# Casting q, k and v on ScalarE in layer 2, and loading the last tokens one tail ahead, in a sliding-window attention with an MLP

## The chip, the core and the metric

The kernel runs on one core of one Trainium2 chip. The metric is the time of one execution on the device in microseconds (us). The core has five engines, each with an instruction stream of its own that it runs in order: TensorE (PE in the profile; its weight loads are shown as PEld), VectorE (DVE), ScalarE (ACT), GpSimd (POOL) and SyncE (SP), which here only issues DMA transfers. Streams meet only where one waits for another's semaphore.

## The reference

Batch 8, 8 heads, 576 positions, head size 64, in float32. Attention looks back over a window of 64 positions; its result, with the heads side by side (512 columns), is normalised and goes through a two-layer MLP of hidden size 2048, with a residual.

```
scores = (q @ k^T) / sqrt(64);  keep 0 <= i - j < 64, else -1e9
x      = softmax(scores) @ v                         # [8, 8, 576, 64] -> [8, 576, 512]
xn     = (x - mean(x)) / sqrt(var(x) + 1e-6) * g_ln
out    = x + relu(xn @ w_ch1) @ w_ch2                # 512 -> 2048 -> 512
```

## The kernel before

**Groups and periods.** The positions 0 to 511 of each batch row are one group (g = 0 to 7), four blocks of 128 tokens each. The last 64 positions of each row, the tails, are put together as a ninth group (g = 8): block i of it, "tail i", holds the last 64 tokens of rows 2i and 2i + 1. A loop over g runs the MLP of group g while the attention of group g + 1 is worked out and the inputs of group g + 2 are loaded, cast to float16 and transposed. One turn of the loop is called a period here. Periods 2 to 5 are the steady ones; in periods 6 and 7 there is no further full group to prepare, and the tails are prepared and attended to instead. Period 8 is the MLP of the tails alone.

**Units and slots.** From period 2 on, the MLP of a group is 30 units on TensorE. Units 0 to 15 are layer 1: four matmuls of 128x512 (`hps`), and a Relu on ScalarE that writes `hrT`. Units 16 to 29 are layer 2, done with seven products of half-size blocks (`product`, n = 1, 2, 6, 5, 7, 3, 4, two token halves each) into the banks X, Y and Z, with sums of `hrT` prepared by VectorE (`presum`, the tiles `sw`) and added into the output tile `osb` by VectorE (`post`). X is used four times in a row, so each time TensorE waits until VectorE has read it. All other work is hung behind a unit with `at(unit, function, arguments)`: after each unit the functions in its slot are called, and the order of these calls is the order of the instructions on every engine. Nothing reorders them afterwards, except that the engines run apart as far as semaphores allow.

**Attention steps in the slots.** `s_mm(g, j)` does the scores of block j on TensorE, followed (or one unit later) by two exps on ScalarE; `s_mask` multiplies the mask in on VectorE; `b_step` multiplies by v on TensorE and does the division and the statistics on VectorE; `r_step` does 1/sqrt(var + eps) as two small instructions on ScalarE; `z_step` normalises on VectorE; `x_step` transposes z into `zT` by a DMA transpose from SP's queue, and `zt_step` does the same on TensorE. The next period's layer 1 reads `zT`.

**Inputs.** `load_qk` and `load_v` issue the loads of group g + 2 from SP at the start of period g. `cast_q` and `cast_v` cast them on GpSimd, one instruction for each half of q and of k (128x1024) and one for each quarter of v (128x512). To keep GpSimd from running them too early, `pace(t)` puts a one-column copy of some tile in front, so that the cast waits for that tile. In the steady periods the casts of q and k stand in slots 3, 5, 8 and 10, those of v in 18, 20, 22 and 25. `x_main` transposes the cast q and k, half by half, by three DMA transposes from SP each, in slots 13 and 22. `make_vB` copies v with a shift of 64 positions by two DMAs from GpSimd. The float32 buffers of q and k (`qk32_0`, `qk32_1`) are two deep, that of v (`v32`) one deep.

**Tails.** `load_tail(i)` loads q, k and v of tail i in six DMAs, q, k, v for each of its two rows, into the same buffers. `cast_tail` casts them on GpSimd in three parts (q, k, v), paced; `x_tail` transposes q and k by one DMA transpose each. The table `TAILS` gives the slots: tail 0 is loaded in slot 0 of period 6, and the load of tail i + 1 stands in the slot of `x_tail(i)`, behind it.

Of the kernel before, what the change touches and what calls it, by code (L numbers as in the profile page):

```python
# [10 lines left out]
FP32 = mybir.dt.float32  # L11
# [7 lines left out]
def kernel(  # L19
# [10 lines left out]
    nc = tc.nc  # L30
# [3 lines left out]
    SM = 512  # L34
# [60 lines left out]
    def load_tail(i):  # L95
        tq = p_in.tile([128, H, D], FP32, tag="qk32_0", name=f"tq32_{i}")
        tk = p_in.tile([128, 2, H, D], FP32, tag="qk32_1", name=f"tk32_{i}")
        tv = p_in.tile([128, 2, H, D], FP32, tag="v32", name=f"tv32_{i}", bufs=1)
        tail32[i] = (tq, tk, tv)
        for r in range(2):  # L100
            b = 2 * i + r
            nc.sync.dma_start(out=tq[64 * r:64 * r + 64], in_=q[b, :, SM:S, :].rearrange("h s d -> s h d"))
            nc.sync.dma_start(out=tk[:, r], in_=k[b, :, S - 128:S, :].rearrange("h s d -> s h d"))
            nc.sync.dma_start(out=tv[:, r], in_=v[b, :, S - 128:S, :].rearrange("h s d -> s h d"))

    def cast_tail(i, part):
        if part == 0:
            tail16[i] = (p_in.tile([128, H, D], FP16, tag="qk16_0", name=f"tq16_{i}"),
                         p_in.tile([128, 2, H, D], FP16, tag="qk16_1", name=f"tk16_{i}"))
            nc.gpsimd.tensor_copy(out=tail16[i][0], in_=tail32[i][0])  # L110
        elif part == 1:
            nc.gpsimd.tensor_copy(out=tail16[i][1], in_=tail32[i][1])
        else:
            vt = p_va.tile([128, 2, H, D + 1], FP16, tag=("vA", "vB")[i % 2], name=f"vt_{i}")
            vT[i] = vt
            nc.gpsimd.memset(vt[:, :, :, D:D + 1], 1.0)
            nc.gpsimd.tensor_copy(out=vt[:, :, :, 0:D], in_=tail32.pop(i)[2])
# [5 lines left out]
    def cast_q(b, x, half):  # L123
        t = qk32.pop((b, x, half))
        dst = p_in.tile([128, 8, 2, D], FP16, tag=f"qk16_{x}", name=f"qk16_{x}_{b}_{half}")
        qk16[(b, x, half)] = dst
        if b >= NPE and x == 1:
            nc.gpsimd.tensor_copy(out=dst[:, :].rearrange("p a e d -> p (a e d)"), in_=t)
            return
        j = 2 if b < 2 else 4  # L130
        nc.gpsimd.tensor_copy(  # L131
            out=dst[:, :].rearrange("p (a j) e d -> p a e j d", j=j),
            in_=t[:, :].rearrange("p (a e j d) -> p a e j d", e=2, j=j, d=D),
        )
# [14 lines left out]
    def cast_v(b, c0, c1):  # L149
        nc.gpsimd.tensor_copy(out=vA[b][:, c0:c1, :, 0:D], in_=v32[b][:, c0:c1])  # L150
# [494 lines left out]
    def rest_of_loads():  # L645
        for i in range(8):
# [13 lines left out]

    TAILS = {
        6: ((0, load_tail, 0), (8, cast_tail, 0), (13, x_tail, 0), (13, load_tail, 1), (21, cast_tail, 1),
            (24, x_tail, 1), (24, load_tail, 2), (21, s_mm, 8, 0), (22, s_mask, 8, 0), (26, b_step, 8, 0)),
        7: ((0, x_step, 8, 0), (0, s_mm, 8, 1), (2, s_mask, 8, 1), (4, b_step, 8, 1), (7, x_step, 8, 1),
            (1, cast_tail, 2), (6, x_tail, 2), (6, load_tail, 3), (9, s_mm, 8, 2), (11, s_mask, 8, 2),
            (13, b_step, 8, 2), (16, x_step, 8, 2), (13, cast_tail, 3), (17, x_tail, 3),
            (20, s_mm, 8, 3), (21, s_mask, 8, 3), (24, b_step, 8, 3), (28, zt_step, 8, 3)),
    }
    for g in range(NGRP):
# [18 lines left out]
        def steps(bg, bj, ub, us, sg, sj):  # L688
            if us is not None:
                score(us, bg, bj)  # L690
            late = ub < 15
            at(ub, b_step, bg, bj)
            if sj < 4:
                score(ub, sg, sj)
            at(ub + 1 + late, r_step, bg, bj)
            at(ub + 2, z_step, bg, bj)
            at(ub + 3, x_step, bg, bj)
# [78 lines left out]
        for i, f, *p in TAILS.get(g, ()):  # L776
# [10 lines left out]
            elif f is cast_tail:  # L787
                for part in range(3):
                    u = i + (0, 1, 3)[part]
                    if u < 16:  # L790
                        at(u, lambda u=u: pace(hrTs[g][:, u, 0:1]))
                    elif part == 1:
                        at(u, lambda: pace(rss[(b, 3)]))
                    at(u, cast_tail, p[0], part)
            else:
                at(i, f, *p)
        if 0 < g and b + 1 < B:
# [19 lines left out]
            else:  # L817
                at(3, alloc_qkT, n)
                for u, x, half in ((3, 0, 0), (5, 1, 0), (8, 0, 1), (10, 1, 1)):
                    at(u, lambda u=u: pace(hrTs[g][:, u, 0:1]))  # L820
                    at(u, cast_q, n, x, half)
                at(13, x_main, n, 0)
                at(22, x_main, n, 1)
                at(18, alloc_v, n)
                at(18, alloc_vB, n)
                for u, c, t in ((18, 0, lambda: rss[(b, 2)]), (20, 1, lambda: oo_of[g][0][:, 0, 0:1]),
                                (22, 2, lambda: rss[(b, 3)]), (25, 3, lambda: oo_of[g][1][:, 0, 256:257])):
                    at(u, lambda t=t: pace(t()))
                    at(u, cast_v, n, c, c + 1)
                at(26, make_vB, n)  # L830
# [37 lines left out]
```

## Time and profile before

| | |
|---|---|
| runs | 325.7, 330.42, 326.16, 333.08 us; median 328.29 us |
| the profiled execution | 325.7 us, of which the span from first to last instruction is 324.0 us |
| mean granted clock of TensorE | 0.973 |
| busy: PE | 297.2 us (92%) |
| busy: PEld | 186.6 us (58%) |
| busy: DVE | 201.9 us (62%) |
| busy: ACT | 158.6 us (49%) |
| busy: POOL | 130.8 us (40%) |
| DMA | 61.55 MB, mean 190 GB/s |
| casts of q and k on POOL (L131, L128) | 32 of 128x1024, 1073 and 1109 ns each |
| casts of v on POOL (L150) | 32 of 128x512, 783 ns each |

Shares are of the span. Matmuls are pipelined, so a busy PE isn't a PE at its peak. A row such as `PE sc L284 <- DMA tkT<-tk: 6.9, 2, 4.2` reads: the instructions of PE that write `sc`, in line 284, waited for a DMA from `tk` to `tkT`, 6.9 us in all, two times, the longest 4.2 us. Tiles are named without their buffer numbers: `hps` and `hrT` are layer 1's sums and result, `sc` the scores, `pt` their exps, `xps` the product with v, `rs` the 1/sqrt, `z` the normalised tokens, `tqT` and `tkT` the transposed q and k of a tail. "Granted clock" is the share of TensorE's full clock that it was given.

### The profile page before, as it was taken

Reading aid. Unit: us, or ns where it says so; the run is one execution under the profiler, and the core shown is the slowest. Engines: PE = TensorE matmul, PEld = TensorE weight load, DVE = VectorE, ACT = ScalarE, POOL = GpSimd, SP = SyncE. Lnnn points to the kernel's source line nnn. Section 1 sums busy time; section 2 is a strip of 40 time slices with the busy share of each in tenths; the row PEclk is TensorE's granted clock in tenths of the full one; section 3 lists DMA queues with packets and bytes.
Section 4 is the critical chain, followed back from the end, with each engine's and each line's share of the span. In section 5 each row is a group of like instructions: output and inputs, shape, how many; then the busy total and the mean of one; then the engine's idle time right before and its main releaser. Section 6 shows DMA issues by size and latency. Waiting matters only on the chain.

```text
span 324.0 us, 7255 instructions
## 1 busy us (share of the span) xinstructions
PE 297.2 (92%) x2907; PEld 186.6 (58%) x2907; DVE 201.9 (62%) x348; ACT 158.6 (49%) x325; POOL 130.8 (40%) x215
## 2 busy tenths in 40 slices
PE   5779998999999989999998999999999949599993
PEld 2446443866744567458645764685478425485582
DVE  0655319377876994698389829973898416371361
ACT  2699751765938801870385048406831725106600
POOL 3676755942754435352435343542504143001000
PEclk9899999999999999999999999999999968789999
DMA  7999899999989857997999699969989996303005
GB/s 178 253 369 342 301 281 264 300 274 241 160 178 281 145 75 171 323 183 119 191 294 188 113 190 292 183 133 252 145 163 149 283 159 94 67 0 131 0 2 130
DMA packets 140002, 61.55 MB, mean 190 GB/s; under 512 B 117072, under 2 KB 132944, under 8 KB 139968
## 3 DMA queue, kind: packets, MB, share of 16 engines
q1 hardware_dynamic: 135792, 49.17, 73.0%
q0 software_dynamic: 3216, 11.39, 12.1%
q10 hardware_dynamic: 960, 0.53, 0.6%
q8 instruction: 23, 0.38, 0.5%
q14 instruction: 11, 0.09, 0.1%
HBM read 38.80 MB, written 9.44 MB: 149 GB/s over the span
## 4 chain that ended last, share of the span: by engine, by line
PE 62%; DVE 14%; DMA 6%; ACT 6%; issue 5%; SPq 5%; POOL 1%; POOLq 0%; DVEq 0%
PE hps L429 23%; PE wX L505 12%; PE wZ L505 7%; PE hph L466 5%; DMA qk<-in_q_dram 4%; PE ch L442 4%; DVE z L357 3%; PE sc L284 3%; PE ch L480 3%; PE xps L327 3%; DVE stats L335 2%; DVE xn L333 2%; DVE sw L419 2%; DVE osb L520 2%; DMA tkT<-tk 2%
## 5 line engine op out<-in xcount | busy, mean ns | idle before, releaser
L429 PE MATMUL hps<-zT,w1g 128*128 128x512 f16 x480 | 113.3, 385 | 0.1
L433 ACT ACTIVATE hrT<-hps 128x512 f16<-128x512 f32 x120 | 71.5, 596 | 59.3 <-PE hps L429 50.8
L429 PEld LDWEIGHTS <-w1g 128*128 128x128 f16 x480 | 45.3, 99 | 54.0 <-issue 7.0
L505 PEld LDWEIGHTS <-sw 128*128 128x128 f16 x448 | 44.6, 100 | 11.8 <-issue 5.4
L311 DVE TENSOR_TENSOR pt<-pt,mask 128x1024 f16<-128x1024 f16 x32 | 24.5, 766 | 31.0 <-ACT pt L304 18.6
L505 PEld LDWEIGHTS <-hrT 128*128 128x128 f16 x336 | 32.4, 98 | 5.4
L346 ACT ACTIVATE rs<-mv,epst 128x1 f32<-128x1 f32 x36 | 10.7, 298 | 46.2 <-DVE mv L337 46.2
L131 POOL CAST qk<-qk 128x1024 f16<-128x1024 f32 x22 | 23.5, 1073 | 22.6 <-DMA qk<-in_q_dram 18.4
L357 DVE TENSOR_SCALAR z<-xn,mv,rs 128x512 f16<-128x512 f32 x32 | 25.7, 802 | 4.5 <-ACT rs L347 4.3
L419 DVE TENSOR_TENSOR sw<-hrT 128x1024 f16<-128x1024 f16 x28 | 20.7, 740 | 11.5 <-ACT hrT L433 11.5
L390 POOL DMA_DIRECT2D out_dram<-osb x20 | 13.2, 663 | 34.7 <-DVE osb L520 23.3
L150 POOL CAST vA<-v 128x512 f16<-128x512 f32 x32 | 24.9, 783 | 2.5 <-DMA v<-in_v_dram 2.4
L335 DVE BATCH_NORM_STATS2 stats<-xn 128x6 f32<-128x512 f32 x36 | 25.0, 695 | 1.2
L333 DVE TENSOR_TENSOR xn<-xps,rcp 128x512 f32<-128x512 f32 x36 | 24.9, 691 | 1.2
L304 ACT ACTIVATE pt<-sc 128x512 f16<-128x512 f32 x32 | 17.4, 595 | 15.7 <-PE sc L284 15.3
L298 ACT ACTIVATE pt<-sc 128x512 f16<-128x512 f32 x40 | 23.8, 594 | 1.8 <-PE sc L284 0.4
L363 POOL CAST tok<-hrT 128x1 f32<-128x1 f16 x28 | 9.3, 331 | 37.4 <-ACT hrT L433 34.2
L466 PE MATMUL hph<-zT,w1g 128*128 128x256 f16 x192 | 23.9, 273 | 0.4 <-ACT zT L374 0.2
L520 DVE TENSOR_TENSOR osb<-wX,xn 128x512 f32<-128x512 f32 x21 | 14.4, 686 | 11.7 <-PE wX L505 11.7
L327 PEld LDWEIGHTS <-pt 128*64 128x64 f16 x576 | 12.3, 111 | 14.3 <-issue 5.7
L466 PEld LDWEIGHTS <-w1g 128*128 128x128 f16 x192 | 17.8, 98 | 3.9 <-issue 0.8
L442 PE MATMUL ch<-w2s,hrT 128*128 128x512 f16 x80 | 19.8, 380 | 0.0
(80 smaller groups left out, 402.9 us busy)
## 6 DMA issues: line engine op xcount, KB each, us to landing
qk<-in_q_dram SPq DMA_DIRECT2D x16, 512.0 KB, 8.4
v<-in_v_dram SPq DMA_DIRECT2D x32, 256.0 KB, 6.0
w2s<-in_moe_w_ch_dram SPq DMA_DIRECT2D x12, 512.0 KB, 7.6
out_dram<-osb POOLq DMA_DIRECT2D x12, 512.0 KB, 6.3
qk<-in_k_dram SPq DMA_DIRECT2D x20, 256.0 KB, 7.8
qk<-in_k_dram SPq DMA_DIRECT2D x6, 512.0 KB, 6.9
w1s<-in_moe_w_ch_dram SPq DMA_DIRECT2D x4, 512.0 KB, 7.2
out_dram<-osb POOLq DMA_DIRECT2D x8, 256.0 KB, 6.0
```

The lines of the kernel that those rows point to most:

```text
L150: nc.gpsimd.tensor_copy(out=vA[b][:, c0:c1, :, 0:D], in_=v32[b][:, c0:c1])
L298: nc.scalar.activation(out=pt[:, par].rearrange("k h w (p j) -> k (h w) p j", j=4), in_=sc[:, :].rearrange("k h w (j p) -> k (h w) p j", j=4),
L311: nc.vector.tensor_tensor(out=ptv, in0=ptv, in1=mb, op=ALU.mult)
L333: nc.vector.tensor_tensor(out=xn, in0=xps[:, :, 0:D], in1=rcp_b, op=ALU.mult)
L335: nc.vector.bn_stats(out=stats, in_=xn.rearrange("p h d -> p (h d)"))
L357: nc.vector.tensor_scalar(out=z, in0=x, scalar1=mv[:, 0:1], scalar2=rss[(g, kb)][:, 0:1], op0=ALU.subtract, op1=ALU.mult)
L419: nc.vector.tensor_tensor(out=S[i], in0=a, in1=b, op=op)
L429: nc.tensor.matmul(out=hps, lhsT=w1g[:, kc, 128 * hc:128 * (hc + 1)], rhs=zT[g][:, kc, :], start=(kc == KCS[0]), stop=(kc == KCS[-1]),)
L433: nc.scalar.activation(out=hrT[:, hc, :], in_=hps, func=AF.Relu, bias=0.0, scale=1.0)
L442: nc.tensor.matmul(out=ch[kb], lhsT=hrT[:, hc, 128 * kb:128 * (kb + 1)], rhs=w2s[:, hc, :], start=(hc == 0), stop=(hc == NHC - 1),)
L466: nc.tensor.matmul(out=hps[:, e], lhsT=w1g[:, kc, 128 * hc:128 * (hc + 1)], rhs=zT[g][:, kc, 256 * half:256 * half + 256], start=(kc == KC ...
L505: nc.tensor.matmul(out=xyz[bank][:, t], lhsT=lhsT, rhs=rhs, start=bool(first and t == 0 and hc == 0), stop=(t == 1 and hc == 7), skip_grou ...
```

## The change

In the steady periods (2 to 5) the casts of q, k and v are issued to ScalarE (`nc.scalar.copy`) instead of GpSimd, without `pace`, and in other slots: q and k in 16, 16, 17 and 19, v in 21 to 24. `x_main` goes to the slots 18 and 21, `make_vB` to 25. Of block 3 of each group, `r_step` and `z_step` stand one slot later.

For the tails, `load_tail` is split: part 0 loads q and k (first both rows of q, then both of k), part 1 loads v. The loads are hung one tail further ahead: q and k of tail 1 stand in slot 6 of period 6, before `x_tail(0)` in slot 10; those of tail 2 in slot 15, before `x_tail(1)` in 18; those of tail 3 in slot 23, before `x_tail(2)` in 25. The casts of tails 1 and 2 go to ScalarE in layer 2 of period 6; those of tails 0 and 3 stay on GpSimd, paced. Two blocks of tail scores, `s_mm(8, 0)` and `s_mm(8, 1)`, stand in period 6 (slots 15 and 27) instead of one, and the last tail's `zt_step` on TensorE becomes an `x_step`.

```diff
+    def load_tail(i, part):
+        if part == 0:
+            tail32[i] = (p_in.tile([128, H, D], FP32, tag="qk32_0", name=f"tq32_{i}"),
+                         p_in.tile([128, 2, H, D], FP32, tag="qk32_1", name=f"tk32_{i}"))
+            tq, tk = tail32[i]
+            for r in range(2):
+                nc.sync.dma_start(out=tq[64 * r:64 * r + 64], in_=q[2 * i + r, :, SM:S, :].rearrange("h s d -> s h d"))
+            for r in range(2):
+                nc.sync.dma_start(out=tk[:, r], in_=k[2 * i + r, :, S - 128:S, :].rearrange("h s d -> s h d"))
+        else:
+            tv = p_in.tile([128, 2, H, D], FP32, tag="v32", name=f"tv32_{i}", bufs=1)
+            tail32[i] += (tv,)
+            for r in range(2):
+                nc.sync.dma_start(out=tv[:, r], in_=v[2 * i + r, :, S - 128:S, :].rearrange("h s d -> s h d"))
...
+    def cp(act, out, in_):
+        if act:
+            nc.scalar.copy(out=out, in_=in_)
+        else:
+            nc.gpsimd.tensor_copy(out=out, in_=in_)
...
     TAILS = {
-        6: ((0, load_tail, 0), (8, cast_tail, 0), (13, x_tail, 0), (13, load_tail, 1), (21, cast_tail, 1),
-            (24, x_tail, 1), (24, load_tail, 2), (21, s_mm, 8, 0), (22, s_mask, 8, 0), (26, b_step, 8, 0)),
-        7: ((0, x_step, 8, 0), (0, s_mm, 8, 1), (2, s_mask, 8, 1), (4, b_step, 8, 1), (7, x_step, 8, 1),
-            (1, cast_tail, 2), (6, x_tail, 2), (6, load_tail, 3), (9, s_mm, 8, 2), (11, s_mask, 8, 2),
-            (13, b_step, 8, 2), (16, x_step, 8, 2), (13, cast_tail, 3), (17, x_tail, 3),
-            (20, s_mm, 8, 3), (21, s_mask, 8, 3), (24, b_step, 8, 3), (28, zt_step, 8, 3)),
+        6: ((0, load_tail, 0, 0), (0, load_tail, 0, 1), (6, load_tail, 1, 0), *tail_casts(0, False, 8, 9, 10),
+            (10, x_tail, 0), (10, load_tail, 1, 1), *tail_casts(1, True, 16, 17, 18), (18, x_tail, 1),
+            (15, s_mm, 8, 0), (16, s_mask, 8, 0), (26, b_step, 8, 0),
+            (15, load_tail, 2, 0), (21, load_tail, 2, 1), (23, load_tail, 3, 0),
+            *tail_casts(2, True, 24, 25, 26), (25, x_tail, 2),
+            (27, s_mm, 8, 1), (28, s_mask, 8, 1)),
+        7: ((0, x_step, 8, 0), (1, load_tail, 3, 1), (2, b_step, 8, 1), (2, s_mm, 8, 2), (4, s_mask, 8, 2),
+            (5, x_step, 8, 1), (7, b_step, 8, 2), (10, x_step, 8, 2), *tail_casts(3, False, 5, 6, 8), (8, x_tail, 3),
+            (12, s_mm, 8, 3), (14, s_mask, 8, 3), (17, b_step, 8, 3), (20, x_step, 8, 3)),
     }
...
-            at(ub + 1 + late, r_step, bg, bj)
-            at(ub + 2, z_step, bg, bj)
+            at(ub + 2, r_step, bg, bj)
+            at(ub + 2 + (not late), z_step, bg, bj)
...
-                for u, x, half in ((3, 0, 0), (5, 1, 0), (8, 0, 1), (10, 1, 1)):
-                    at(u, lambda u=u: pace(hrTs[g][:, u, 0:1]))
-                    at(u, cast_q, n, x, half)
-                at(13, x_main, n, 0)
-                at(22, x_main, n, 1)
+                for u, x, half in ((16, 0, 0), (16, 1, 0), (17, 0, 1), (19, 1, 1)):
+                    at(u, cast_q, n, x, half, True)
+                at(18, x_main, n, 0)
+                at(21, x_main, n, 1)
...
-                for u, c, t in ((18, 0, lambda: rss[(b, 2)]), (20, 1, lambda: oo_of[g][0][:, 0, 0:1]),
-                                (22, 2, lambda: rss[(b, 3)]), (25, 3, lambda: oo_of[g][1][:, 0, 256:257])):
-                    at(u, lambda t=t: pace(t()))
-                    at(u, cast_v, n, c, c + 1)
-                at(26, make_vB, n)
+                for c in range(4):
+                    at(21 + c, cast_v, n, c, c + 1, True)
+                at(25, make_vB, n)
```

## The prediction

> **What bounds the kernel now.** I began with the 40-slice table of the page. TensorE is busy in nearly every slice except two near the end, and there its clock drops as well:
>
> ```profile
> PE   5779998999999989999998999999999949599993
> PEclk9899999999999999999999999999999968789999
> ```
>
> So TensorE sets the time, and there is a hole. Next came the table by stage, cut at the first `hps` matmul of each period g (g=2 to g=8; columns: length, busy time of PE, PEld, DVE, ACT, POOL, clock, DMA share, GB/s):
>
> ```profile
> 95.48:127.07 31.59, 30.11 (x306) 19.23 (x304) 25.31 (x43) 14.74 (x32) 14.05 (x23) 1.00 0.83 168
> 127.07:157.04 29.97, 29.67 (x304) 19.05 (x302) 22.18 (x39) 14.66 (x32) 12.90 (x24) 1.00 1.00 203
> 157.04:188.70 31.66, 30.26 (x308) 19.37 (x306) 23.54 (x39) 14.55 (x32) 13.72 (x24) 1.00 0.91 201
> 188.70:219.62 30.92, 30.07 (x307) 19.20 (x304) 23.48 (x39) 14.66 (x32) 14.23 (x24) 1.00 0.98 202
> 219.62:250.22 30.60, 30.60 (x337) 19.61 (x335) 24.13 (x44) 16.21 (x36) 8.60 (x14) 1.00 1.00 179
> 250.22:292.32 42.10, 34.30 (x279) 20.83 (x277) 20.19 (x35) 14.34 (x30) 8.64 (x16) 0.84 0.61 119
> ```
>
> Period 7 takes 42.1 us with fewer PE instructions than period 6, which takes 30.6 and has no idle time. Periods 2 to 5 lose 1.48, 0.30, 1.40 and 0.85 us, 4.0 together. The waits of PE name the two causes:
>
> ```profile
> PE sc L284 <- DMA tkT<-tk: 6.9, 2, 4.2
> PE wX L505 <- DVE osb L520: 3.9, 7, 1.0
> ```
>
> The first is the scores of a tail waiting for its transposed keys. The second is the X bank of layer 2 waiting for VectorE. The timeline shows the first (its SP queue, then PE):
>
> ```profile
> 261.31 1.23 SPq L254 DMA_TRANSPOSE tkT<-tk  x1
> 262.60 0.62 SPq L102 DMA_DIRECT2D tq<-in_q_dram  x1
> 264.44 0.61 PE L284 MATMUL sc<-tqT,tkT 64*128 64x64 f16 x16 [4.21 <-DMA tkT<-tk]
> 281.01 0.61 PE L284 MATMUL sc<-tqT,tkT 64*128 64x64 f16 x16 [2.73 <-DMA tkT<-tk]
> ```
>
> Tail i+1 is loaded only behind the transposes of tail i, so load, cast and transpose of one tail follow each other within one tail's time.
>
> **What the change removes in the tail.** The waits are 4.21 + 2.73 = 6.94 us. After each the granted clock is 0.50: in the two-microsecond windows from 264.4 to about 269.2, and from 281.0 to about 286.3. A wide matmul there takes 0.43 us instead of 0.21, so half of 4.8 and half of 5.3 is lost: 5.05. Sum 12.0. Check: period 6 has five score and five value groups (0.41 and 0.45 us), period 7 three of each, so period 7 should last 30.6 - 2 x 0.86 = 28.9; it lasts 13.2 more, which also holds 0.86 of waiting for VectorE. Moving `s_mm(8, 1)` from period 7 to 6 only moves PE work. `zt_step(8, 3)` (four transposes on PE, 0.39 us) becomes a DMA transpose issued at unit 20; `zT` transposes land in 3.4 us and ten units of some 0.9 remain, so it is covered and PE gains 0.4. Without that cover it would cost up to its 3.4.
>
> **What it moves in the steady periods.** Four q/k casts and four v casts leave GpSimd for ScalarE. No row has the very cast on ScalarE. The nearest are a 1024-wide copy (1008 ns), a 64-partition f32-to-f16 cast of 512 (619), and a 512-wide cast with a per-partition scale (722). I take 1.0 and 0.62: 4 x 1.0 + 4 x 0.62 = 6.5 us a period; bounds 6.4 and, by doubling 722, 4 x 1.45 + 4 x 0.72 = 8.7. What hides them is ScalarE's idle time in layer 2:
>
> ```profile
> 212.02 0.29 ACT L346 ACTIVATE rs<-mv,epst 128x1 f32<-128x1 f32 x1 [5.34 <-DVE mv L337]
> 220.73 0.60 ACT L433 ACTIVATE hrT<-hps 128x512 f16<-128x512 f32 x1 [8.19 <-PE hps L429]
> ```
>
> q0, k0, q1 (3.0, at most 4.4) go into the 5.34; k1 and v (3.5, at most 4.3) into the 8.19. Cost zero. Behind them on ScalarE wait `r_step` of block 3, then z on VectorE, then the X bank: if q0 to q1 took over 5.3 us, the excess would go to PE. On SP, `x_main(n, 0)` moves from unit 13 to 18, past the zT transpose of block 2; `x_main(n, 1)` from 22 to 21, still behind that of block 3. Each is three DMA transposes of some 1.26 us on SP. In period 5 SP was held by loads until 205.3 and reached `x_main(n, 0)` only at 209.2; the casts on ScalarE, starting behind the last Relu at 206.7, give k0 at 208.7 (all four halves had landed: the last q/k cast ran at 204.6). So SP's order is new but its times are not: 209.9 to 213.7 for the first half, z of block 3 to 215, then the second, where 215.8 was. `make_vB` on GpSimd now waits for the last v cast (216.1 instead of 217.9), and the output stores behind it go no later. The r and z steps of block 3 go one unit later, z behind one `sw` of 0.69 instead of ahead of it: nothing, as both stand ahead of the same `osb`.
>
> **What the moved casts free.** VectorE is slowed while GpSimd casts:
>
> ```profile
> 168.41 1.04 POOL L128 CAST qk<-qk 128x1024 f16<-128x1024 f32 x1 [0.92 <-DMA qk<-in_k_dram]
> 168.76 1.24 DVE L419 TENSOR_TENSOR sw<-hrT 128x1024 f16<-128x1024 f16 x1
> 231.22 0.66 DVE L419 TENSOR_TENSOR sw<-hrT 128x1024 f16<-128x1024 f16 x1
> ```
>
> The second and third are the same operation, with a cast beside it and without. z takes 0.86 in the mean of periods 2 to 5 and 0.55 alone: 16 x 0.31 = 4.9 us, and `sw` and the masks add some 3.7. PE can get back only what it lost, 4.0 in all. Period 6, where no cast stands beside layer 2 until late, lost nothing, so I take most of it, 3.0; bounds 0 (VectorE would still be late) and 4.0.
>
> **New waits in the tail, the part that costs.** These are estimates on period 6's own times.
> 1. SP now has ten loads in period 6 (tail 0, then q and k of tail 1) ahead of `x_tail(0)`. Six took 221.2 to 228.4, 1.2 each; the later six 0.78 each. Ten take 7.8 to 12: until 229 to 233. Then z of block 0 (1.3), tqT and tkT (1.25 each), and 3.1 to land: tkT at 235.0 to 239.0. `s_mm(8, 0)` is now at unit 15, 236.6. Wait: 0 to 2.4; I take 1.0.
> 2. v of tail 1 is loaded behind that, lands near 242.5, and its cast (1.0) is ahead of `r_step(7, 3)` on ScalarE, which was at 241.8. About 1.7 late, most of it inside wait 1 and PE's lead: 0.5, bounds 0 and 2.
> 3. v of tail 2 goes out behind the zT transpose of block 3 (244.7 to 246.4), two issues of 0.6, 5.3 to land: 251 to 253. Its cast stands on ScalarE ahead of r of (8, 0), the two exps of `s_mm(8, 1)` and the first Relu of period 7, 1.0 + 0.5 + 1.1 us of work; that Relu was at 251.5 and comes at 253.5 to 255.5. PE has two banks of lead, 1.8 us, and its own delay of 1.5. I take 1.5; bounds 0 and 3.
>
> Sum 3.0, bounds 0 and 7.4. `s_mm(8, 2)` and `(8, 3)` follow their transposes by about 2 and 0.8 us by the same reckoning: zero, but thin for the last.
>
> Here a threshold matters. The trace has PE at half clock after a wait of 2.73 us, which followed 0.86 of idling; waits up to 1.0 in the steady periods left it at 1.00. I price a lone wait under 2.7 at its length only. The Trainium skill, "TensorE: Matmul & The Clock Gate", Part 1, puts the drop at an idle window of about 3.4 us. By it only waits of that length would be charged the 2.65 of half clock, and the sum would be the same 3.0; the row is stricter, and I let the row decide in the rivals.
>
> **Sum.** 324.0 - 12.0 - 0.4 - 3.0 + 3.0 = 311.6 us of span. The profiled execution took 325.7, 1.7 around its span: 313.3. The median of the four runs (325.7 to 333.08) lies 2.6 above that execution, so the predicted median is 315.9.
>
> **Rivals.**
> - Forecast, 316: chance 0.64. Own range 308.4 (4.0 regained, no new wait, the 0.86 of period 7 gone too, no offset of the median) to 320.3 (new waits 7.4).
> - The tail wait is moved, not removed: one new wait, tkT of tail 0 or of tail 3, passes 2.7 and halves the clock, adding some 3 + 2.65. Speaking for it: 0.8 of slack at tail 3. Against: every tail has half a period more. 316 + 5.7 = 321.6. Chance 0.21, half of it past the 2% line.
> - Slower: the second q half comes late in every steady period. Its transpose was issued at 215.8, takes 3.3 to land (219.1) and is read at 220.6: 1.5 us of slack. If the casts on ScalarE or SP's new order delay it by more than 1.5, PE waits at unit 0. A delay of 4.5 gives 3 of wait and 2.65 at half clock in each of four periods, 22.6: 338.5. It beats the gain in the tail from 3.1 a period on. Against: SP reached it by loads, not by casts. Chance 0.11.
> - The change doesn't shorten the tail: loads of one tail ahead crowd the DMA (share 1.35 around 230) and land as late as before. Only the 3.0 and 0.4 remain: 324.9. Against: the DMA share is 0.20 to 0.32 from 232 to 236. Chance 0.04.
>
> A run can tell about 2% of this kernel from no change, so faster means under 321.7. Faster: 0.64 + 0.11 = 0.75; same: 0.10 + 0.04 = 0.14; slower 0.11. The range, 308.4 to 325.0, adds the moved wait and the tail that isn't shortened to the forecast's own.
>
> **What will show it.** Right: period 7 near 30 us, clock 1.00 through it, `tkT` gone from PE's waits, z near 0.55. Wrong: a wait of `sc` for `qkT` at unit 0, `rs` late behind a cast, or `hrT` of period 7 waiting for a v load. The forecast falls if period 7 still shows clock 0.5, or if periods 2 to 5 exceed 31 us.

## The result, and the profile after

The changed kernel takes 321.75 us (median of 12 runs, 320.57 to 324.47). The kernel before took 326.16 in the same comparison (17 runs). The ratio is 0.990 (95% interval 0.986 to 0.994): the change gains 1.0%, where 3.8% was forecast (315.9 against 328.29). The time lies inside the range given, but the gain is under the 2% that the forecast named as its line. Here and below a median is of all executions, while a ratio and its interval leave out those more than 1.5% above the fastest of the same kernel. The profiled execution took 320.86 us, of which 319.1 are its span, at a mean granted clock of 0.982.

The 40-slice table of the changed kernel has the same two rows as before:

```profile
PE   6689999999999999999799979999958979999993
PEclk9999999999999999999999989999995999999999
```

The two lean slices of period 7 are gone; lean ones stand earlier, in period 6, and the clock has its gap there, with a small dent (8) before it. The table by stage tells where each piece is. Columns as before: length, busy time of PE, PEld, DVE, ACT, POOL, clock, DMA share, GB/s; one row for each of the periods 2 to 7.

```profile
93.50:123.70 30.20, 29.84 (x305) 19.22 (x304) 23.28 (x43) 20.56 (x40) 3.08 (x7) 1.00 0.88 178
123.70:154.60 30.90, 29.89 (x306) 19.21 (x305) 21.68 (x40) 20.56 (x40) 3.68 (x8) 1.00 0.96 201
154.60:185.20 30.60, 29.94 (x305) 19.41 (x306) 20.29 (x38) 20.66 (x40) 3.35 (x7) 1.00 1.00 203
185.20:218.60 33.40, 31.34 (x306) 19.73 (x305) 20.98 (x39) 20.77 (x40) 3.48 (x8) 0.95 0.98 193
218.60:257.00 38.40, 33.84 (x354) 21.33 (x352) 24.15 (x44) 21.12 (x43) 5.39 (x12) 0.91 1.13 190
257.00:287.70 30.70, 28.66 (x259) 18.50 (x258) 19.32 (x34) 13.60 (x29) 6.25 (x10) 1.00 0.51 104
```

Against the rows of before, period 7 fell by 11.40 us (42.10 to 30.70), as forecast. Period 6 grew by 7.80 (30.60 to 38.40). Periods 2 to 5 changed by -1.39, +0.93, -1.06 and +2.48, 0.96 longer in all, where 3.0 less was forecast. Period 8 is 0.28 shorter. Another 1.98 lies ahead of period 2, in code that is the same; there, profiled executions of the unchanged code differ by as much (period 2 starts at 93.6 and at 95.5 in two kernels with it). The sum is 4.9, the difference of the spans.

PE's waits name what came in:

```profile
PE sc L292 <- DMA tkT<-tk: 6.6, 3, 4.6
PE sc L292 <- DMA qkT<-qk: 2.7, 2, 2.1
PE hps L437 <- DMA zT<-z: 1.0, 1, 1.0
PE wX L513 <- DVE osb L528: 0.4, 1, 0.4
```

The last row is the relief of VectorE: the X bank waited 3.9 us in seven places before, and 0.4 in one now. The first three rows were not there or were elsewhere, and all three are DMA transposes. Of the waits for `tkT`, 4.56 us stand in period 6, for tail 0, and 2.0 in period 7, in two places.

The timeline of period 6 shows the first wait, from SP's queue (rows marked SPq) to TensorE:

```profile
219.88 2.29 SPq L101 DMA_DIRECT2D tq<-in_q_dram  x2
...
230.14 1.30 SPq L103 DMA_DIRECT2D tk<-in_k_dram  x2
231.57 2.98 SPq L390 DMA_TRANSPOSE zT<-z  x1
234.65 2.23 SPq L261 DMA_TRANSPOSE tqT<-tq  x1
236.97 1.26 SPq L262 DMA_TRANSPOSE tkT<-tk  x1
240.28 0.61 PE L292 MATMUL sc<-tqT,tkT 64*128 64x64 f16 x16 [4.56 <-DMA tkT<-tk]
```

SP issues ten loads without a pause until 231.5. Then z of block 0 and tq take 2.98 and 2.23 us each, where a transpose alone takes 1.2 to 1.3. GpSimd had ended the cast of the keys at 232.4, so their transpose went out 4.6 us behind its cast, and then landed in 3.3. The keys are there at 240.2, and TensorE had come to them at 235.7. After the wait the clock is at one half. TensorE's busy time in the period is 3.24 longer than before (30.60 to 33.84), 0.4 of it for the tail scores that the change moved here, and some 2.8 for the clock. With the wait of 4.56 that is the growth of the period.

The steady periods show the other two waits, here at the change from period 3 to period 4, and in the last row early in period 5:

```profile
149.31 1.22 SPq L390 DMA_TRANSPOSE zT<-z  x1
150.06 0.54 POOL L180 DMA_DIRECT2D vB<-vA  x1 [23.49 <-ACT vA L129]
150.62 2.64 SPq L245 DMA_TRANSPOSE qkT<-qk  x1
154.61 1.02 PE L437 MATMUL hps<-zT,w1g 128*128 128x512 f16 x4 [1.02 <-DMA zT<-z]
188.46 0.40 PE L292 MATMUL sc<-qkT,qkT 64*128 64x64 f16 x8 [2.06 <-DMA qkT<-qk]
```

z of block 3 is issued at 149.31, and `make_vB`'s first copy goes out beside it at 150.06. z lands after 5.1 us, and the second q half, issued at 150.62, after 5.8. A period later the copies go out 0.7 behind z and 0.6 ahead of the q half; z takes 3.3, the q half 6.1 us, and TensorE waits 2.06 for it; the clock of period 5 is 0.95, another 1.7 us. In periods 2 and 5 the copies go out more than 1.0 behind the q half, and there z takes 2.4 and the q half 3.1 and 3.2.

### The profile page after: what moved, and what is told of

Read it like the earlier page. It is cut to its first block, busy times and chain, and to the rows that moved or that the text cites. A ratio compares the mean times of both kernels' runs of the same rounds, so it can differ in the third digit from the quotient of the medians.

```text
span 319.1 us, 7196 instructions
## 1 busy us (share of the span) xinstructions
PE 294.5 (92%) x2903; PEld 185.8 (58%) x2903; DVE 191.9 (60%) x348; ACT 186.7 (59%) x362; POOL 84.4 (26%) x142
## 4 chain that ended last, share of the span: by engine, by line
PE 67%; DMA 9%; DVE 9%; ACT 6%; SPq 5%; issue 2%; POOL 0%; DVEq 0%; ACTq 0%
PE hps L437 29%; PE wX L513 10%; PE wZ L513 5%; PE hph L474 5%; PE ch L450 4%; DMA qkT<-qk 4%; PE sc L292 4%; DMA tkT<-tk 3%; PE xps L335 3%; PE ch L488 3%; PE wY L513 3%; DMA qk<-in_k_dram 2%; DVE stats L343 2%; DVE xn L341 2%; DVE osb L528 2%
## 5 line engine op out<-in xcount | busy, mean ns | idle before, releaser
L513 PEld LDWEIGHTS <-sw 128*128 128x128 f16 x448 | 43.8, 98 | 5.6 <-issue 0.5
L319 DVE TENSOR_TENSOR pt<-pt,mask 128x1024 f16<-128x1024 f16 x32 | 23.4, 732 | 30.8 <-ACT pt L306 17.6
L513 PEld LDWEIGHTS <-hrT 128*128 128x128 f16 x336 | 33.3, 101 | 6.4
L180 POOL DMA_DIRECT2D vB<-vA x6 | 3.2, 535 | 101.0 <-ACT vA L129 100.4
L427 DVE TENSOR_TENSOR sw<-hrT 128x1024 f16<-128x1024 f16 x28 | 18.8, 671 | 12.1 <-ACT hrT L441 12.1
L365 DVE TENSOR_SCALAR z<-xn,mv,rs 128x512 f16<-128x512 f32 x32 | 19.0, 594 | 8.1 <-ACT rs L355 8.0
L131 POOL CAST qk<-qk 128x1024 f16<-128x1024 f32 x16 | 17.0, 1069 | 13.7 <-DMA qk<-in_q_dram 7.7
L338 DVE RECIPROCAL rcp<-xps 128x8 f32<-128x8 f32 x36 | 7.4, 204 | 17.2 <-PE xps L335 17.1
```

The source lines that it names most:

```text
L319: nc.vector.tensor_tensor(out=ptv, in0=ptv, in1=mb, op=ALU.mult)
L365: nc.vector.tensor_scalar(out=z, in0=x, scalar1=mv[:, 0:1], scalar2=rss[(g, kb)][:, 0:1], op0=ALU.subtract, op1=ALU.mult)
L513: nc.tensor.matmul(out=xyz[bank][:, t], lhsT=lhsT, rhs=rhs, start=bool(first and t == 0 and hc == 0), stop=(t == 1 and hc == 7), skip_grou ...
```

## The experiments

Each was compared with runs of the kernel before on its own chip; ratios are against those. A profile is of a single execution; those of e4 and e6 took 326.4 and 326.8 us, 2.5 above their medians, and that of e7 took 324.1, 5.8 above the shortest of its four. Diffs are against the changed kernel where nothing else is said.

### The two halves alone (e1, e2)

e1 has the steady half of the change with the tails of before; e2 has the tails of the change with the steady periods of before.

```diff
 e1:  load_tail, cast_tail, TAILS as in the kernel before
 e2:  cast_q, cast_v, x_main, make_vB, r_step, z_step in the slots and on the engine of before
```

> Only the steady half of the change: casts of periods 2 to 5 on ScalarE, tails as in the kernel before. By the trace of the changed kernel the four periods last 125.0 us against 124.1 before: VectorE's relief of some 3 us is spent on waits of the scores for qkT (0.65 and 2.06, with the half clock behind the second) and 1.02 for zT. Theory: 0 to +1 us against before, ratio about 1.00, tail unchanged (period 7 about 42 us). Rival: the waits are an accident of one execution, then the relief shows: 3 us faster, 0.99.

> Only the tail half: loads one tail ahead, casts of tails 1 and 2 on ScalarE, steady periods as before. Theory (the tail wait is moved to period 6): period 7 falls from 42 to about 31 us, period 6 rises from 31 to 36 or 38 with a wait of s_mm(8, 0) for tkT of 3 to 4.6 us and half clock behind it: 3 to 6 us faster than before, 0.98 to 0.99. Rival: the wait of 4.56 us is due to TensorE being earlier through the steady half; then the wait is under 2.4 us, the clock holds, and the gain is 9 us or more, 0.97.

Measured: e1 328.0 us (ratio 0.995, 0.985 to 1.004), e2 322.65 (0.991, 0.988 to 0.995). e1's ratio comes from two of its ten executions, 321.37 and 326.06, so a gain of up to 1.5% stays possible; what its trace shows is the waits of the changed kernel once more, 0.9 for `zT` and 0.7 and 2.4 for `qkT`. The tail half shows about the gain of the whole change. In e2 TensorE still waits 3.7 us for tail 0's keys, so the wait is not made by TensorE being earlier alone; in these two traces that accounts for at most the 0.9 by which 4.56 exceeds 3.7.

### Moving single steps away from the collision (e3, e4, e5, e8)

```diff
 e3: +                at(25, lambda: pace(oo_of[g][1][:, 0, 256:257]))
                      at(25, make_vB, n)
 e4: -            (15, s_mm, 8, 0), (16, s_mask, 8, 0)
     +            (20, s_mm, 8, 0), (21, s_mask, 8, 0)
 e5: -            ((16, 0, 0), (16, 1, 0), ...)  cast_q on ScalarE;  at(18, x_main, n, 0)
     +            first halves in slots 3 and 5 on GpSimd, paced;    at(13, x_main, n, 0)
 e8:  e4 and e5 together, and the v casts of tails 1 and 2 on GpSimd
```

> The changed kernel with the two DMAs of make_vB held back by a one-column copy of the osb tile that is written behind unit 25. Theory (collision: in the two periods with a wait those DMAs went out 0.6 us ahead of the transpose of the second q half, which then took 5.8 and 6.1 us to land, and 3.1 and 3.2 in the two where it was ahead): all four land in 3.1 to 3.5, no wait for qkT, clock 1.00 at the start of period 5, 3 to 5 us faster than the changed kernel, about 0.98 of before. Rival (SP's order: the first half behind the zT transpose of block 2 makes it late): landing and waits stay, no gain.

> The changed kernel with s_mm(8, 0) and its mask in slots 20 and 21 instead of 15 and 16; loads and casts untouched. Theory: tkT of tail 0 lands near 240, TensorE reaches unit 20 near 240.5, so the wait of 4.56 us and the half clock behind it (2.9) go; but the cast of v of tail 1 then waits for its load until 243.3 ahead of r_step(7, 3), and 2 to 4 us come back as a wait of VectorE and the X bank. Net 3 to 5 us faster than the changed kernel. Rival: the wait for tkT follows the scores to wherever they stand (transposes paced by TensorE): no gain.

> The changed kernel, but in the steady periods the first halves of q and k are cast on GpSimd again in units 3 and 5, and their transposes go out at unit 13 as before; the second halves and v stay on ScalarE. Theory A (the second q half is late because block 3's z transpose and it stand on SP behind the first half's three transposes, which the change moved from unit 13 to unit 18: 145.32 to 149.21 in period 3, while z of block 3 was ready at 147.47): z's transpose goes out 1 to 2 us sooner, the q half too, the waits qkT (2.7) and the period's first zT (1.0) go, no half clock in the steady periods, periods 2 to 5 at 29.8 to 30.9 each; about 317 to 319 in all, against 320.9 for the profiled run of the changed kernel. Theory B (the q half lands late because of the copies that build vB, 5.8 to 6.1 in place of 3.2): the landing stays at 5 to 7 in periods 3 and 4 and a wait of 1 to 2 us stays; 320 to 322. Theory C (GpSimd's casts cost VectorE what the change relieved): z returns from 594 ns to over 700 and the periods to 31; 321 to 323.

> Three edits on the changed kernel together: the first half of q and k cast on GpSimd in units 3 and 5 (its transposes at 13), the score of tail 0's block at unit 20 in place of 15, and the v casts of tails 1 and 2 on GpSimd. If the causes are the ones read in the trace (the bunch of transposes on SP, the score ahead of its keys, and a v cast on ScalarE ahead of period 7's Relus, which waited 2.8 us where the score stood late), each of the last periods is 30 to 33 and the steady ones 30 to 31: 312 to 316. If a transfer is late wherever the score stands (late score alone gave 323.85), a tkT wait of 2 to 4 us stays in period 6 or 7: 318 to 322.

Measured: 325.3 (0.996, 0.990 to 1.002), 323.85 (0.991, 0.986 to 0.996), 323.2 (0.990, 0.977 to 1.002) and 324.94 (0.998, 0.993 to 1.003). None beats the changed kernel. With vB held back, the q half lands in 3.2 and 3.1 us in periods 4 and 5, but in period 3 in 7.2, with vB's copies 0.9 us behind it, and TensorE waits 3.06 there; tail 0's keys hold it up for 5.1. In e4 tail 0's keys are in time, and a wait of 2.8 comes at the start of period 7: its first Relus (`hrT`) stand behind the v cast of tail 2 on ScalarE. In e5 the earlier slot did nothing: SP was busy with loads, and in period 3 the first half's transposes went out at 145.5, where the changed kernel had 145.3. In e8 TensorE waits 2.5 and 5.8 for keys of later tails. So whichever step was moved, some transpose or load was late somewhere else. That suggested that the order on one queue is not the whole of it.

### SP's queue, or the transfers themselves? (e6, e7)

```diff
 e6: -            (6, load_tail, 1, 0), ... (10, x_tail, 0), (10, load_tail, 1, 1)
     +            (10, x_tail, 0), (10, load_tail, 1, 0), (10, load_tail, 1, 1)
 e7:  in load_tail: nc.sync.dma_start -> nc.gpsimd.dma_start
```

> The changed kernel, but the four q and k loads of tail 1 go to SP behind tail 0's transposes, not ahead of them. Theory A (tail 0's transposes are late because SP is still issuing loads: ten from 219.88 to 231.5, of which these four took 227.93 to 231.44): tkT of tail 0 is issued about 3.5 us sooner, at 233 to 234, the wait of 4.56 falls to 0 to 1.5, the clock in period 6 stays full, period 6 at 31 to 34 in place of 38.5; the loads' 3.5 us come back further on as waits of ScalarE for tq and tk of tail 1, behind which r_step of block 3 and the exps stand, 0 to 3 us. 314 to 319 in all. Theory B (the casts or the transposes themselves are late, not the queue): tkT still lands at 239 to 240, the wait stays at 3.5 to 4.6; 320 to 322.

> The changed kernel, but all loads of the tails are issued by GpSimd in place of SP. Theory A (SP's queue is what makes tail 0's transposes late): SP issues only transposes in period 6, z of block 0 and tqT go out when they are ready (casts of tail 0 ended at 231 to 233.6), tkT lands at 233 to 236 and the wait falls from 4.56 to under 1; period 6 at 31 to 33; 313 to 317. Theory B (the loads' data or the casts come late whoever issues them): the wait stays over 3; 319 to 323. Theory C (GpSimd's issuing stands behind its own casts and buffer waits, so tails 1 to 3 load later): the wait of tail 0 goes and one of 2 to 6 us comes at tail 2 or 3, or at ScalarE's cast of v; 318 to 324.

Measured: e6 324.3 (0.992, 0.987 to 0.997); e7 326.24, but from 318.35 to 336.53 in four runs, so its time decides nothing. e6's trace has no wait for tail 0's keys. Their cast ends at 237.04, their transpose goes out at 237.07 and lands in 3.1, just as TensorE comes to them (240.32). In the changed kernel 4.6 us lay between cast and transpose. The transposes of z and tq are quick in e6, too: 1.23 and 1.36 us on SP, where the changed kernel had 2.98 and 2.23. The DMA share at that time is 0.07 to 0.39 (231 to 237 us) in e6, and 1.37 and 1.35 (231 to 235) in the changed kernel. But e6 gains no more than the changed kernel. Its longest wait is the forecast's third one, `hps` for `hrT` at the start of period 7, 3.3 us, and at the start of period 6 this execution waits 2.7 for `zT` and 1.25 for `qkT`.

In e7's trace the keys are late in another way. Its timeline has this on SP and on TensorE:

```profile
233.62 5.30 SPq L262 DMA_TRANSPOSE tkT<-tk  x1
245.06 0.61 PE L292 MATMUL sc<-tqT,tkT 64*128 64x64 f16 x16 [8.88 <-DMA tkT<-tk]
```

SP issued no load in that stretch, and the keys' transpose went out as soon as they were cast, 3.35 us sooner than in the changed kernel. Yet its issue took 5.30 us in place of 1.26, it landed 11.4 us after, and the wait grew to 8.88. So both count. In the changed kernel the keys lose their time on SP, behind loads and two slow transposes, and four loads fewer ahead of them are enough. But a free queue alone does not bring a transpose in on time: in e7, a single execution, the loads that GpSimd had issued were under way in place of SP's.

### Taking transfers away (e9, e14; e10, e13, e17)

e9 and e14 leave the same ten output stores out of the changed kernel and out of the kernel before. e10 and e13 keep all work but build vB by seven engine casts of 64x512 a period from the loaded v: e10 on GpSimd, e13 on ScalarE. e17 does the latter in the kernel before.

```diff
 e9, e14:
     -                stores.append((cur[0], nc.gpsimd, dst, oo[p]))
     +                if not 2 <= g <= 6:
     +                    stores.append((cur[0], nc.gpsimd, dst, oo[p]))
 e13 (e10: the same casts by nc.gpsimd.tensor_copy, in slots 22 to 25; e17: in slots 26 and 27 of the kernel before):
     -                at(18, alloc_vB, n)
     +                at(18, init_vB, n)
     -                at(25, make_vB, n)
     +                for c in range(4):
     +                    at(25, vB_cur, n, c, 0)
     +                for c in range(3):
     +                    at(26, vB_prev, n, c, 0)
```

> The changed kernel without the output stores of periods 2 to 6 (two of 512 KB each; the output is left unwritten there). Nothing else moves. Theory A (the 16 DMA engines are the second bound: share 0.88, 0.96, 1.00, 0.98 and 1.13 in periods 2 to 6 of the changed kernel, so a transpose that is issued in time lands 5 to 7 us later): with 10 stores fewer the share falls by 0.1 to 0.15, the second q half lands within 3.1 to 3.5 us in every period, the qkT and zT waits go (2.7 and 1.0), the tkT wait in period 6 falls to under 3, the clock stays full in the steady periods; periods 2 to 5 at 30 to 30.6, period 6 at 31 to 35; 312 to 317 in all. Theory B (the order of SP's queue alone makes them late, whoever else uses the DMA engines): the q half lands at 5 to 6 in periods 3 and 4, the waits of 1 to 2 us stay, tkT stays at 3.5 to 4.6; 320 to 322.

> The kernel before without the output stores of periods 2 to 6, the same ten that e9 left out. Theory A (before the change the DMA engines are not what sets the time; TensorE waits for VectorE in the steady periods and for tail transposes in period 7): the steady periods stay at 30.3 to 31.5, the hole in period 7 stays within 2 us of 10, 322 to 325.5; the change is then worth 8.5 to 12 where the DMA engines have room, as forecast (12.4 of span). Theory B (stores bound both alike): it falls by 6 to 8, to 317 to 320, and the change is worth 4 to 6 with or without room.

> The changed kernel, but in the steady periods vB is built by GpSimd straight from the loaded v (seven casts of 64x512 a period, in units 22 to 25), in place of the two DMA copies of 260 and 195 KB. Theory A (DMA engines full): 0.45 MB less a period takes 0.04 to 0.08 off the share, the second q half lands in 3.1 to 4 us in periods 4 and 5 and perhaps 3, the qkT wait falls below 1 and with it the half clock; periods 3 to 5 at 30 to 31; 318 to 320.5. Theory B (the lateness is not from DMA traffic): landing 5 to 7 and a wait of 2 us in one of the periods; 321 to 323. Theory C (GpSimd's casts slow VectorE again, next to block 3's z): z over 650 ns and zT waits of 1 to 2 us; 321 to 324.

> The changed kernel, vB built in the steady periods by ScalarE (seven casts of 64x512, in units 25 and 26, behind the v casts), in place of the DMA copies. Seven times some 0.55 is 3.9 us of ScalarE; it stood idle 4.95 to 6.2 ahead of the next period's first Relu. Theory A (DMA engines full, and e10's longer steady periods, 31.4 to 31.6, were GpSimd slowing VectorE: sw 792 ns for 665): periods 2 to 5 at 29.8 to 30.7, z at 544 ns, no wX wait, share at 0.9 or less, 316.5 to 319.5. Theory B (ScalarE's 3.9 us don't fit and hold up the first Relu): waits of TensorE for hrT of 0.5 to 2 in each period; 320 to 324.

> The kernel before with vB built by ScalarE in units 26 and 27, in place of the DMA copies. If it behaves as without stores (e14): steady periods 30.7 to 31.6, the two tail waits stay, 320 to 324; the change is then worth 5 to 8 us (e13 is 315.75 in its own job). If ScalarE's 3.9 us hold up the next period's Relus here, since GpSimd's v casts end later than ScalarE's (217.9 against 216.1): waits for hrT of 1 to 2 us a period, 326 to 332.

Measured: e9 313.64 (ratio 0.963, 0.960 to 0.967) and its control e14 320.56 (0.981, 0.974 to 0.989). e13 315.75 (0.967, 0.961 to 0.973) and its control e17 323.38 (0.993, 0.990 to 0.997). e10 320.8 (0.986, 0.982 to 0.990).

Without the stores the changed kernel is 6.9 us faster than the kernel before without them; with vB made by ScalarE, 7.6 us. As they stand the two differ by 4.4. These pairs ran on different chips. By the ratios, each to its own chip, the change is worth 1.0% as it stands, 1.8% without the stores (an estimate from the two intervals: 1.0 to 2.7) and 2.7% with vB by ScalarE (2.0 to 3.4). So the change is worth more where GpSimd issues no copies of vB; without the stores it probably is, but the intervals overlap. e14 fell between its two theories: the kernel before gains from fewer stores too (its longest tail wait is 2.7, not 4.2), though its steady periods stay at 30.7 to 31.6.

e13's table by stage has the steady periods (2 to 5) as the forecast wanted them:

```profile
94.40:124.60 30.20, 29.84 (x305) 19.19 (x304) 23.28 (x43) 24.39 (x47) 2.38 (x7) 1.00 0.89 174
124.60:154.30 29.70, 29.70 (x306) 19.27 (x305) 20.98 (x39) 24.51 (x48) 2.75 (x8) 1.00 0.97 193
154.30:184.10 29.80, 29.80 (x307) 19.33 (x306) 21.00 (x39) 24.50 (x47) 2.85 (x8) 1.00 1.00 196
184.10:213.80 29.70, 29.70 (x307) 19.27 (x305) 20.99 (x39) 24.51 (x47) 2.74 (x8) 1.00 0.94 195
```

TensorE has no idle time in periods 3 to 5. The four take 119.4 us, against 123.1 in e17: 3.7 us of relief. The DMA share, the column before the last, is no lower than in the changed kernel, and in e9 it was 1.00 and 1.04 in two periods. My expectation of a fall by 0.1 failed, so the mean share of a period does not tell how late a transpose lands. What differs is who shares the engines at that moment. The list of DMA queues for 150 to 157 us (packets, MB, share of the 16 engines), in the changed kernel:

```profile
q0 software_dynamic: 243, 0.94, 60.6%
q1 hardware_dynamic: 1606, 0.39, 38.6%
```

and in e13:

```profile
q1 hardware_dynamic: 2377, 0.58, 71.1%
q0 software_dynamic: 104, 0.43, 29.9%
```

q0 holds the transfers that GpSimd issues (vB's copies and the output stores), q1 those of SP. Without vB's copies q0 has half the share, and SP's queue gets 2377 packets through in place of 1606. Counted from the issue of z of block 3 over 5.3 us (149.3 to 154.6, and 148.4 to 153.7 in e13), it gets 1047 through in the changed kernel and 2315 in e13. z of block 3 landed in 2.4 us in e13, where it took 5.1. The q half behind it still took 4.7 in e13 in this period, with no wait; the kernel before had 4.8.

e10 separates the price of where the casts run. Its steady periods are even, but at 30.6 to 31.7 us, with wX waiting 4.9 us in eight places. The `sw` sums of VectorE, in the changed kernel and then in e10 (both 94 to 220 us; the mean ns stands behind the busy time):

```profile
L427 DVE TENSOR_TENSOR sw<-hrT 128x1024 f16<-128x1024 f16 x16 | 10.6, 664 | 0.0
```

```profile
L432 DVE TENSOR_TENSOR sw<-hrT 128x1024 f16<-128x1024 f16 x16 | 12.7, 792 | 0.0
```

GpSimd's casts in layer 2 slow VectorE, and the X bank waits again. That is the very cost that the change had taken out. ScalarE has the room: in e13 the seven casts took 3.84 us and the next Relu still waited for TensorE.

### Spreading the tails (e11, e12, e15, e16) and the steady half with room (e18)

e11 takes tail 1's loads behind tail 0's transposes and leaves all of tail 3 and most of tail 2 to period 7; all tail casts are on GpSimd. e12 and e15 add vB by GpSimd and by ScalarE. e16 is e15 with the scores of tails 2 and 3 two slots later. e18 is e1 with vB by ScalarE.

```diff
 e11 ('pool': on GpSimd, not paced):
+        6: ((0, load_tail, 0, 0), (0, load_tail, 0, 1), *tail_casts(0, False, 8, 9, 10),
+            (10, x_tail, 0), (10, load_tail, 1, 0), (10, load_tail, 1, 1), *tail_casts(1, 'pool', 17, 19, 21),
+            (20, x_tail, 1), (17, s_mm, 8, 0), (18, s_mask, 8, 0), (26, b_step, 8, 0),
+            (22, load_tail, 2, 0), (27, load_tail, 2, 1)),
+        7: ((0, x_step, 8, 0), (1, s_mm, 8, 1), (3, s_mask, 8, 1), *tail_casts(2, False, 1, 2, 4), (3, x_tail, 2),
+            (3, load_tail, 3, 0), (5, load_tail, 3, 1), (5, b_step, 8, 1), (8, x_step, 8, 1),
+            (8, s_mm, 8, 2), (10, s_mask, 8, 2), (12, b_step, 8, 2), (15, x_step, 8, 2),
+            *tail_casts(3, False, 9, 10, 13), (12, x_tail, 3),
+            (17, s_mm, 8, 3), (18, s_mask, 8, 3), (20, b_step, 8, 3), (23, x_step, 8, 3)),
 e16: in period 7, s_mm(8, 2) at 10, s_mask 12, b_step 13, x_step 16; s_mm(8, 3) at 19, s_mask 20, b_step 21, x_step 24
```

> The changed kernel with its tails spread: tail 1's loads behind tail 0's transposes, tail 2's q and k from unit 22 of period 6 and its v from unit 27, its transposes, its score and all of tail 3 in period 7; all tail casts on GpSimd. Theory A (the load of the DMA engines in period 6 is what makes the keys late: 43 engine-us stand in 38.4 us there after the change, where 30.7 stood before, and period 7 has 16 in 30.7): the tkT wait in period 6 is under 1.5, the share there falls to 1.0 or less, period 6 at 31 to 34, period 7 at 30 to 33; 313 to 319. Theory B (whatever is moved out of period 6 returns as a wait in period 7, since each tail's chain of load, cast, transpose and landing is some 15 us long): period 6 at 31 to 34 and period 7 at 34 to 38; 319 to 323.

> Both: tails spread and vB built by GpSimd. If DMA load is the second bound, the gains add: 311 to 317; if each only moves a wait, 319 to 323.

> e11's spread tails and vB by ScalarE. If the gains add: steady periods 29.8 to 30.7, periods 6 and 7 at 32 to 33 each: 313 to 316.5. If spreading only moves a wait, 317 to 320.

> As the one before, and the scores of tails 2 and 3 two units later in period 7 (their blocks one unit later), since TensorE waited 1.49 and 1.59 for tkT there in e12. If the transposes are late by their chain alone, these waits go and period 7 is 1 to 3 us shorter: 312 to 315. If block 3's z comes late for period 8 instead, the wait moves to its first matmul: within 1 us of the kernel without this.

> The change's steady half alone (the tails as before), with vB built by ScalarE. If the relief of VectorE is real and only the DMA engines kept it from the clock: steady periods at 29.7 to 30.2 against 30.7 to 31.6 of the kernel before without stores, 3 to 5 us under e17: 316 to 320. If the steady half is worth nothing whatever the DMA engines have to do (e1: 328.0): within 1 us of e17.

Measured: e11 319.57 (0.979, 0.973 to 0.985), e12 318.3 (0.978, 0.974 to 0.982), e15 313.42 (0.959, 0.952 to 0.966), e16 309.68 (0.949, 0.943 to 0.956). By these ratios the gains of the spread tails (e11) and of vB by ScalarE (e13) add in e15. e16 beats both kernels by far: 5.1% under the kernel before. Its table by stage, periods 5 to 7:

```profile
183.70:213.40 29.70, 29.70 (x306) 19.26 (x305) 20.98 (x39) 24.50 (x47) 2.74 (x8) 1.00 0.96 197
213.40:244.40 31.00, 30.72 (x338) 19.83 (x337) 24.47 (x45) 16.36 (x36) 8.02 (x13) 1.00 0.98 171
244.40:276.50 32.10, 29.28 (x275) 18.67 (x273) 20.71 (x34) 13.75 (x28) 10.04 (x17) 1.00 0.79 152
```

The clock is full, and periods 6 and 7 cost 63.1 us where they cost 72.7 before the change and 69.1 after it. The forecast's own terms give 72.7 - 12.0 - 0.4 + 3.0 = 63.3, though for another order of the tails, so the near agreement confirms no single term. What is left are two waits for tkT in period 7, 1.3 and 1.1 us, too short to cost clock.

e18 took 319.8 us (0.984, 0.975 to 0.993), 3.6 under e17 on the same chip. The steady half alone, which gained nothing in e1, gains its relief once vB's copies are gone.

## Why the prediction was wrong, step by step

- **What bounds the kernel.** Right for TensorE, and incomplete. The other limit is how soon a DMA transpose lands beside other transfers. The forecast's table shows DMA shares of 0.91 to 1.00 in periods 3 to 6; that column was read for the tail only, and for the old traffic: the rival of the crowded loads was set aside because the share was 0.20 to 0.32 from 232 to 236, and with ten loads ahead it was 1.37 and 1.35 from 231 to 235.
- **What is removed in the tail (12.0).** Right: period 7 fell by 11.40 with its clock at 1.00. The clock term of 5.05 fits as well: TensorE's busy time in period 7 fell by 5.64, of which some 0.8 is work that went elsewhere (one score group and the four transposes). 42.10 us at a mean clock of 0.84 look like 6.7, but half clock began 2.0 and 1.6 us before the ends of the two waits, where there was nothing to slow down. What the forecast had at zero are waits for later tails: 2.0 of `tkT` stand in period 7 now.
- **Casts on ScalarE at no cost.** Right. A 128x1024 cast took 0.97 to 1.05 us and four v casts 2.18, and in the steady periods the Relus of the next period waited for TensorE, not for a cast.
- **Relief of VectorE (3.0).** The mechanism was right: the mean z in the steady periods fell from 857 to 543 ns, and the size was 3.7 where e13 and e18 left it room (e17 as the control). In the changed kernel it was more than spent, on 3.7 us of waits and 1.6 of half clock. Slack was lost in two ways. The q half of periods 3 and 4 was issued 3.0 and 2.8 us ahead of TensorE's arrival at unit 0, where the kernel before had 4.7 and 4.2; and it took 5.8 and 6.1 to land, not the 3.3 of the forecast. At 3.3 neither would have been waited for. In e13, where TensorE is as early, the lead is 4.7 and 4.2 again. That is the rival of the late q half, in two of the four periods and at 1.7 us (1.02 of it for z) and 2.1 (with half clock), where it had asked for 3 in each.
- **Wait 1 (1.0, bounds 0 to 2.4).** This is the step that failed. The ten loads ended at 231.4, inside the forecast's 229 to 233. Behind them, z, tqT and tkT were priced at 1.25 to 1.3 each from rows in a quiet stretch; the first two took 2.98 and 2.23. And TensorE came 0.9 sooner (235.7, not 236.6). So 4.56, outside the bounds, with some 2.8 of half clock behind it that the term did not hold: 7.4 in place of 1.0.
- **The price of a wait.** "A lone wait under 2.7 at its length only" was wrong. The wait of 2.06 us in period 5 cost 1.7 more.
- **The offset of the median (2.6).** It came from four executions. Over all, the median lies 0.5 above the profiled execution in the kernel before and 0.9 in the changed one, so the miss is larger in the span: 319.1 against 311.6.
- **The sum.** Of these 7.5 us wait 1 makes 6.4, the relief 4.0 (3.0 forecast, 0.96 lost), the waits of period 7 2.0; waits 2 and 3 (2.0), the part ahead of period 2 (1.98) and small differences in periods 6 to 8 take 4.9 off again.
- **Waits 2 and 3 (0.5 and 1.5).** Neither shows in the changed kernel, perhaps because its TensorE was late already. Wait 3 is real: in other kernels the first Relus of period 7 held TensorE up for 2.8 (e4), 3.3 (e6) and 2.5 us (e13).
- **The likeliest case.** The rival in which the tail wait is moved and not removed, with half clock behind it, was given 321.6 us and a chance of 0.21. It is the mechanism that came, and 321.75 was measured; part of that agreement is chance, since relief was lost as well and 1.98 us ahead of period 2 were gained. With z and tqT priced at 2.98 and 2.23, the upper end of wait 1 would have been 2.7 higher, at 5.1, far past the 2.7 from which the forecast charged half clock, and this rival would have had to stand higher.

What remains open is how GpSimd's transfers delay the transposes: by their bytes, by their larger packets, or by their queue. e9, e10 and e13 take all three away together. Nor is it shown what makes the issue of a transpose on SP last 2 to 5 us at times. Why the q half of period 3 landed late in nearly every kernel (4.7 in e13, 7.2 in e3) is not settled either.

## What to carry to other kernels

A slack that was measured before a change does not carry over: work it out again for the new order of issues, above all for transfers that must land before the bounding engine comes. Price a transfer from a row in the same kind of stretch as the one it will land in, and look at who else moves data in those few microseconds; the mean DMA share of a period did not show it here, the share over two microseconds did. A wait that is moved must end short of the lengths that cost clock (none up to 1.92 us did here), or the move gains little.

## What the runs showed of the hardware that I had not expected

The clock does not drop at a fixed length of a wait. I looked at every lone hole of TensorE of 0.8 us and more from period 2 on, in the profiles of both kernels and of all experiments, no other hole being within 11 us. None of some 20 up to 1.92 us cost clock. Of the 12 from 2.06 to 2.94, seven did and five did not: 2.06 and 2.22 did, while 2.32 and 2.94 did not. All 12 from 3.06 on did. The loss comes in portions: half clock lasts 3.4 us or twice that, a loss of 1.7 or 3.4, save for one hole of 8.9 with 5.1. Where half clock begins inside the hole, that part slows nothing down (1.0 of the 3.4 at the wait of 4.21 in the kernel before).

The Trainium skill, "TensorE: Matmul & The Clock Gate", Part 1, speaks of a free-running window of about 3.4 us. The portions agree with it: half clock for one such window would lose 1.7, an estimate from the page's figure. Its "idle window" is not borne out as a whole window without work, since a hole of 2.06 us was enough. That it depends on where a hole falls in the window fits these counts, but no run here shifts a hole of fixed length to test it.

A DMA transpose of the same size landed in 2.4 us with no copy of GpSimd's beside it (z of block 3, e13), and in 5.1 and 3.3 with one close behind it (the changed kernel, periods 3 and 4). With tail loads issued by GpSimd beside it, one took 11.4 (tkT in e7), where 3.3 had sufficed.
